# Tile 0 scored in plain float32, GpSimd rounds the first keys, scales and splits the weights and splits one subtile of tile 1, and the early tiles run in a new order

## The chip, the cores and the metric

One core of a Trainium2 chip runs the kernel. Five engines matter here. TensorE (PE) multiplies matrices. VectorE (DVE), ScalarE (ACT) and GpSimd (POOL) work elementwise. SyncE (SP) issues every DMA, one after another from one queue. Each engine works its own list of instructions in order, and semaphores hold an instruction until what it reads is there and the buffer it writes is free. The metric is the device time of one execution in microseconds. The kernel before takes 1856.12 us (median of three runs, 1855.11 to 1856.93).

## The reference

Attention over pooled keys, then a gated feed-forward layer. B = 4, 12288 queries per batch, C = 128, 768 keys per batch, 1024 hidden columns:

```python
kv_pool = kv.reshape(B, H // r, r, W // r, r, C).mean(axis=(2, 4))   # r = 4
k = v = kv_pool.reshape(B, -1, C) @ w_sr                             # 768 keys
s = (q @ k.transpose(0, 2, 1)) / sqrt(C)
a = exp(s - s.max(-1)); a /= a.sum(-1) + 1e-09
x = a @ v
xk = mu_k * x + (1 - mu_k) * x_prev      # x_prev: x of the query before
xr = mu_r * x + (1 - mu_r) * x_prev
out = sigmoid(xr @ w_r) * (maximum(xk @ w_k, 0) ** 2 @ w_v)
```

## The kernel before

The queries run in 97 tiles: 95 of 512 columns and, at the end, two of 256. A tile of 512 has four subtiles of 128 queries. Per subtile PE makes the scores `S` (128x768 in one of three `big` PSUM buffers), DVE takes the row maximum (`nm`), ACT the exponential and its sum (`ex`), and ACT and DVE split the scaled result into a rounded half and a remainder (`f1`, `f2`, tile `pp`). SP transposes `pp` by DMA into `pT` (`tt`). Then PE makes `px` = values x `pT` (`AV0` to `AV5`, 18 matmuls). From `px` come `xk` and `xr`, each split again. PE makes four blocks of hidden columns from `xk` (`ha`, `hb`, PSUM `ph`), ACT and DVE square them (`r`, `k2`, `kh`, `kl`), PE sums them into `pv` (`va`, `vb`) and makes the gate `pz` (`z`).

Almost every product is made of three narrow ones, from operands split into a high and a low part. For the scores of the first tiles these are `ql` x `kbl` (bfloat16), `qh` x `ksh` (a rounded float32) and `qh` x the second half of `kbl`. `ksh`, `kb` and `kd` are the three steps that make the split keys, `qh` and `ql` those that split the queries, `wh` and `wd` (`wx2` for a third copy) those that split the weights `wk`, `wv`, `wr`.

Before the first score the head loads the weights (`L_wk0` and so on), eight blocks of the first 512 key columns (`L_a0` to `L_a7`, tile `kva`) and five groups of the other 256 (`L_b0` to `L_b4`, tile `kvb`). All thirteen key loads share six buffers (`kv`), so the seventh load waits until the first is used. PE sums the `a` blocks into `pk` (`pa0` to `pa7`, two float32 matmuls each), DVE sums the `b` groups (`ab`), PE multiplies these by the key weights (`pk1`, `pk2`), and ACT writes the keys (`ks0` to `ks2`). The rest of the head finds the largest weight (`wa`, `wc`, `wx` to `wg`), prepares the weights on DVE and ACT (`wb`, `wf`, `wu`, `ws`, `wt`, `we`, `wl`, `wq`, `wp`) and prepares the values (`vh`, `vl`, transposed by `tv`). The `id` steps are fillers: two 128-column float32 matmuls each, of a unit matrix with itself, whose result nobody reads.

The order is a table of numbers. Every step has a due time, in `ONCE` for the head and `EARLY` for tiles 0 to 7, and in `WHEN` (plus a period of 19.3 per tile) after that. `Plan` sorts all steps by due time and issues them. The numbers are not checked against the clock: they set nothing but the order on each engine, and a step late on one engine holds whatever stands behind it there.

Of the kernel before, what the change touches and what calls it, by code (L numbers as in the profile page):

```python
# [23 lines left out]
K_SHIFT = 23  # L24
# [49 lines left out]
def tile_kernel(ctx, tc, qT, kv0a, kv0b, kvw, head, w_k, w_v, w_r, outT):  # L74
# [114 lines left out]
    land, sums = {}, {}  # L189
# [50 lines left out]
    def weights(name, w, hi, lo, place, extra):  # L240
# [94 lines left out]
        for i, (c0, c1) in enumerate(parts):  # L335
            @once(f"wh_{name}{i}")
            def _(i=i, c0=c0, c1=c1):
                act.activation(
                    out=hi[:, c0:c1], in_=st["t", i], func=AF.Copy, scale=gain(name)
                )  # L340

            if ENGINE["wd"] == "P":
                @once(f"wz_{name}{i}")
                def _(i=i):
                    act.activation(
                        out=st["t", i], in_=st["t", i], func=AF.Copy, scale=gain(name)
                    )

            @once(f"wd_{name}{i}")
            def _(i=i, c0=c0, c1=c1):  # L350
                if ENGINE["wd"] == "P":
                    pool.tensor_tensor(
                        out=lo[:, c0:c1], in0=st["t", i], in1=hi[:, c0:c1], op=ALU.subtract
                    )
                else:
                    dve.scalar_tensor_tensor(
                        out=lo[:, c0:c1], in0=st["t", i], scalar=gain(name), in1=hi[:, c0:c1],
                        op0=ALU.mult, op1=ALU.subtract,
                    )

            if extra is not None:
                @once(f"wx2_{name}{i}")
                def _(i=i, c0=c0, c1=c1):
                    pool.tensor_copy(out=extra[:, c0:c1], in_=hi[:, c0:c1])
# [19 lines left out]
    def first_keys(ks):  # L384
# [54 lines left out]

        return pks  # L440
# [35 lines left out]
    def batch_prep(b, i0, res):  # L476
# [22 lines left out]
        for n, (c0, c1) in enumerate(PARTS if not later else []):  # L499
            @at(f"ksh{n}")  # L500
            def _(n=n, c0=c0, c1=c1):
                act.activation(
                    out=put("ksh")[:, c0:c1], in_=pks[n][:, 0:c1 - c0], func=AF.Copy, scale=scale / WIN
                )

            @at(f"kb{n}")
            def _(n=n, c0=c0, c1=c1):
                act.activation(
                    out=put("kbl")[:, 0, c0:c1], in_=pks[n][:, 0:c1 - c0], func=AF.Copy,
                    scale=scale / WIN,  # L510
                )

            @at(f"kd{n}")
            def _(n=n, c0=c0, c1=c1):
                dve.scalar_tensor_tensor(
                    out=put("kbl")[:, 1, c0:c1], in0=pks[n][:, 0:c1 - c0], scalar=scale / WIN,
                    in1=res["ksh"][:, c0:c1].bitcast(F32), op0=ALU.mult, op1=ALU.subtract,
                )
# [16 lines left out]
        def _():  # L535
# [5 lines left out]
            dve.reciprocal(ivs, exs)  # L541

# [54 lines left out]

        @at("sv")
        def _():
            dve.reciprocal(xi, xt)  # L600
            dve.tensor_scalar_mul(sk, xi[:, 2:3], X_TOP)
            dve.tensor_copy(out=put("bk"), in_=xt[:, 2:3])
            for i in range(2):
                dve.tensor_scalar(
                    put("s4")[:, 2 * i:2 * i + 2], mix[:, 2 * i:2 * i + 2], xi[:, i:i + 1], exs,
                    op0=ALU.mult, op1=ALU.mult,
                )
# [17 lines left out]
    def plan_tile(i, b, t0, T, at0):  # L625
# [10 lines left out]
        last = max((f"v{x}{f}" for x in "ab" for f in range(NF // 2)), key=places.get)  # L636
        first = min((f"v{x}{f}" for x in "ab" for f in range(NF // 2)), key=places.get)
# [4 lines left out]
        def at(name):  # L642
            def put(fn):
                plan.add(places[name] + base, name, fn, ("tile", i))
# [94 lines left out]
        def _():  # L739
# [4 lines left out]
            act.copy(out=st["qh"], in_=st["qf"])  # L744
# [23 lines left out]
        def products(S, s, c0, c1):  # L768
            ksh, kbl = bps[b]["ksh"], bps[b]["kbl"]
# [8 lines left out]
        for s in range(NSUB):  # L778
# [61 lines left out]
            if opt["TT"][s] == "P":  # L840
# [15 lines left out]
                def _(s=s):  # L856
                    if "pT" not in st:
                        new("pT")
                    act.copy(out=st["pT"][:, s, 0:NK, :], in_=st[f"pm{s}"][:, 0:NK, :])
# [9 lines left out]

            @at(f"f1{s}")  # L870
            def _(s=s):
                pp = new(f"pp{s}")
                rc = st[f"rc{group[s]}"][:, s:s + 1]
                if opt["F1"][s] == "A":
# [20 lines left out]
        for j in range(NK):  # L895
            @at(f"AV{j}")
            def _(j=j):
                vT = bps[b]["vT"]
                name = f"AV{j}"
                if name == av_first:  # L900
                    st["px"] = take("x", name="px")[:, 0:T]
                for m, (w, a) in enumerate(((0, 1), (1, 0), (0, 0))):
# [78 lines left out]

        for f in range(NF // 2):
# [3 lines left out]
            def _(f=f, halves=halves):  # L986
# [3 lines left out]
                st[f"ph{f}"] = ph  # L990
                for i, fs in halves:
# [17 lines left out]
            def _(f=f):  # L1009
                if opt["KV"][f] in "24":  # L1010
# [73 lines left out]
OPT = {'F1': 'AAAA', 'CAST': 'DD', 'KV': '1123', 'T1': 'D', 'TT': 'DDDD'}  # L1084
EARLY_OPT = [{'TT': 'DDDP'}]
# [7 lines left out]
POOLED = ()  # L1093
ENGINE = {'wd': 'D', 'cz': 'P', 'cv': 'P', 'uz': 'P', 'vl': 'P', 'am': 'D', 'mq': 'A', 'qs': 'P'}
# [7 lines left out]
IDLE = 24  # L1102
# [385 lines left out]
```

## Time and profile before

| | us |
|---|---|
| median of three runs | 1856.12 |
| profiled execution, first to last instruction | 1854.3 |
| PE busy | 1839.3 (99%) |
| DVE busy | 1730.9 (93%) |
| ACT busy | 1743.0 (94%) |
| GpSimd busy | 1133.2 (61%) |
| PE waits named in the trace, sum | 5.8 |

PE is busy in nearly the whole span, but a filler counts as busy too. So a reader has to separate PE time into products that the result needs, fillers, and waits. All named waits of PE but two (0.5 us and 0.2 us) lie before 60 us. The time of a run and the span of the profiled execution differ by 1.8 us here, of which the trace says nothing.

### The profile page before, as it was taken

To read this page: it belongs to the slowest core of one execution; us is meant where nothing else is said; L and a number is where in the kernel's file an instruction comes from. 1 tells how busy PE (TensorE), PEld (TensorE's weight loads), DVE (VectorE), ACT (ScalarE), POOL (GpSimd) and SP (SyncE) were. 2 spreads that over 40 slices of the span, in tenths; PEclk is the share of its full clock that TensorE was granted. 3 is DMA by queue.
4 is the path that set the end of the run, shared out by engine and by line. 5 is a ranking of instruction groups with operands and counts; after the bars stand their busy time and mean duration, and the time that the engine had idled before them with its cause. 6 is when DMAs were issued, how large, how long until landed. Compare 5 with 4: busy or idle time off the path is not lost.

```text
span 1854.3 us, 27743 instructions
## 1 busy us (share of the span) xinstructions
PE 1839.3 (99%) x9079; PEld 912.5 (49%) x9185; DVE 1730.9 (93%) x2811; ACT 1743.0 (94%) x2628; POOL 1133.2 (61%) x875
## 2 busy tenths in 40 slices
PE   9999999999999999999999999999999999999999
PEld 6444454444444444444444444444444444444445
DVE  8999999999999999999999999999998999899898
ACT  6999999999999999999999999999999999999997
POOL 1655565666666566666666666656666666666666
PEclk9999999999999999999999999999999999999999
DMA  7677575656667676656666676747565656555462
GB/s 248 142 154 160 130 166 125 129 128 131 135 138 168 142 159 148 134 118 128 137 127 164 142 170 141 161 103 142 123 136 120 128 128 125 120 109 114 91 126 57
DMA packets 654336, 252.52 MB, mean 136 GB/s; under 512 B 612080, under 2 KB 613104, under 8 KB 654192
## 3 DMA queue, kind: packets, MB, share of 16 engines
q1 hardware_dynamic: 654192, 250.75, 63.1%
q8 instruction: 72, 1.18, 0.3%
q14 instruction: 72, 0.59, 0.1%
HBM read 73.34 MB, written 25.17 MB: 53 GB/s over the span
## 4 chain that ended last, share of the span: by engine, by line
PE 89%; ACT 2%; issue 1%; DVE 0%; DVEq 0%; ACTq 0%
PE ph L39 25%; PE pv L39 24%; PE S L39 19%; PE px L39 18%; PE pz L39 3%; ACT rr L39 0%; ACT kh L39 0%; ACT pp L39 0%; PE pk L39 0%; ACT pe L39 0%; ACT kk L39 0%; ACT S L39 0%; ACT xer L39 0%; DVE pp L39 0%; DVE kk L39 0%
## 5 line engine op out<-in xcount | busy, mean ns | idle before, releaser
L39 POOL TENSOR_TENSOR kl<-kk,kh 128x1024 bf16<-128x1024 f32 (+1 forms) x291 | 617.9, 2124 | 129.4 <-ACT kh L39 112.6
L39 ACT ACTIVATE rr<-ph 128x1024 f32<-128x1024 f32 (+1 forms) x388 | 395.8, 1021 | 80.0 <-PE ph L39 76.8
L39 PE MATMUL px<-pT,vT 128*128 128x512 f16 (+1 forms) x1746 | 391.8, 377 | 2.1 <-DMA pT<-pp 2.1
L39 POOL TENSOR_TENSOR xrl<-xr,xrh 128x512 f16<-128x512 f32 (+1 forms) x97 | 144.9, 1494 | 275.1 <-DVE xrh L39 275.1
L39 ACT ACTIVATE kh<-rr 128x1024 f16<-128x1024 f32 (+1 forms) x291 | 306.5, 1055 | 0.7 <-PE pv L39 0.2
L39 PE MATMUL S<-kf,qh 128*128 128x256 f16 x1264 | 304.3, 326 | 0.0
L39 PE MATMUL ph<-xkh,wkl 128*128 128x512 f16 (+1 forms) x776 | 292.0, 377 | 0.4 <-DVE kk L39 0.2
L39 PE MATMUL pv<-kh,wvl 128*128 128x512 f16 (+1 forms) x776 | 291.9, 377 | 0.1
L39 PE MATMUL ph<-xkh,wkh 128*128 128x512 f16 (+1 forms) x776 | 291.9, 377 | 0.0
L39 PE MATMUL pv<-kh,wvh 128*128 128x512 f16 (+1 forms) x776 | 291.8, 377 | 0.0
L39 DVE SCALAR_TENSOR_TENSOR pp<-pe,rc,pp 128x768 f16<-128x768 f32 x289 | 286.9, 1011 | 0.5 <-ACT pp L39 0.5
L39 PEld LDWEIGHTS <-vT 128*128 128x128 f16 x1746 | 170.4, 98 | 205.9 <-issue 3.1
L39 ACT ACTIVATE pp<-pe,rc 128x768 f16<-128x768 f32 x289 | 263.8, 952 | 1.6 <-DVE rc L39 1.6
L39 DVE TENSOR_SCALAR_CACHE_REDUCE pe<-S,gs 128x768 f32<-128x768 f32 x238 | 238.0, 1015 | 25.5 <-PE S L39 25.4
L39 POOL TENSOR_TENSOR ql<-qf,qh 128x512 f16<-128x512 f32 (+2 forms) x97 | 141.9, 1463 | 195.1 <-ACT qh L39 195.1
L39 ACT ACTIVATE pe<-pe,nm 128x768 f32<-128x768 f32 x265 | 248.0, 936 | 0.3 <-DVE pe L39 0.3
L39 PEld LDWEIGHTS <-wkh 128*128 128x128 f16 x1552 | 151.8, 98 | 178.4 <-issue 0.7
L39 DVE TENSOR_TENSOR kk<-ph,rr 128x1024 f32<-128x1024 f32 (+1 forms) x194 | 233.9, 1206 | 3.9 <-ACT rr L39 3.2
L39 PE MATMUL ph<-xkl,wkh 128*128 128x512 f16 (+1 forms) x776 | 228.6, 377 | 0.0
L39 PE MATMUL S<-kf,ql 128*128 128x256 f16 x632 | 205.9, 326 | 4.1
L39 POOL TENSOR_TENSOR xkl<-xk,xkh 128x512 f16<-128x512 f32 (+1 forms) x97 | 145.1, 1496 | 103.0 <-DVE xkh L39 103.0
L39 PE MATMUL pv<-kl,wvb 128*128 128x512 bf16 (+1 forms) x681 | 193.0, 377 | 0.5
(152 smaller groups left out, 2937.5 us busy)
## 6 DMA issues: line engine op xcount, KB each, us to landing
qf<-qT SPq DMA_DIRECT2D x95, 256.0 KB, 3.6
outT<-o SPq DMA_DIRECT2D x95, 256.0 KB, 3.4
qm<-qT SPq DMA_DIRECT2D x78, 256.0 KB, 3.6
kvt<-kvw SPq DMA_DIRECT2D x36, 512.0 KB, 4.9
pT<-pp SPq DMA_TRANSPOSE x383, 4.0
kva<-kv0a SPq DMA_DIRECT2D x8, 512.0 KB, 9.4
kvb<-kv0b SPq DMA_DIRECT2D x3, 512.0 KB, 6.0
land<-moe_w_k SPq DMA_DIRECT2D x2, 512.0 KB, 6.2
```

Of the source, the lines that this page charges most:

```text
L39: return self.tc.keep_in_program_order(op(*args, **kwargs))
```

## The change

Tile 0 takes its scores from the queries and keys as they are, in plain float32: one product of a 128x128 by 128x768 instead of three, and no `qh` and `ql` for it. The split keys are made by GpSimd from the finished `ks`, one instruction for all 768 columns each, where ACT and DVE made them from PSUM in three parts. The weights are scaled in place by GpSimd (`wz`, new), rounded by ACT (`wh`) and the remainder is taken by GpSimd (`wd`, on DVE before). Subtile 0 of tile 1 is scaled (`f00`, new), rounded and split by GpSimd. `sv` is cut in two (`sw` is its later part). The head and tiles 0 to 7 have new due times, and there are 30 fillers where there were 24. `WHEN` and the last two tiles keep theirs. (Branches of the new code for letters other than "S" in `WHOLE` are not taken.)

```diff
@@ weights
+            @once(f"wz_{name}{i}")
+            def _(i=i):
...
+                    {"P": pool, "D": dve}[ON["wz"]].tensor_scalar(
+                        st["t", i], st["t", i], gain(name), 1.0, op0=ALU.mult, op1=ALU.mult
+                    )
             @once(f"wh_{name}{i}")
             def _(i=i, c0=c0, c1=c1):
-                act.activation(
-                    out=hi[:, c0:c1], in_=st["t", i], func=AF.Copy, scale=gain(name)
-                )
+                COPY[ON["wh"]](out=hi[:, c0:c1], in_=st["t", i])
             @once(f"wd_{name}{i}")
             def _(i=i, c0=c0, c1=c1):
...
+                {"P": pool, "D": dve}[ON["wd"]].tensor_tensor(
+                    out=lo[:, c0:c1], in0=st["t", i], in1=hi[:, c0:c1], op=ALU.subtract
+                )
@@ batch_prep
-        for n, (c0, c1) in enumerate(PARTS if not later else []):
-            @at(f"ksh{n}")
...
+        if not later:
+            @at("ksh")
+            def _():
+                COPY[ON["ksh"]](out=put("ksh"), in_=ks)
+            @at("kb")
+            def _():
+                COPY[ON["kb"]](out=put("kbl")[:, 0, :], in_=ks)
+            @at("kd")
+            def _():
+                {"P": pool, "D": dve}[ON["kd"]].tensor_tensor(
+                    out=put("kbl")[:, 1, :], in0=ks, in1=res["ksh"].bitcast(F32), op=ALU.subtract
+                )
@@ plan_tile, products
+            if "S" in whole:
+                pe.matmul(
+                    S[:, c0:c1], lhsT=st["qf"][:, s * P:(s + 1) * P], rhs=bps[b]["ks"][:, c0:c1],
+                    start=True, stop=True,
+                )
+                return
@@ plan_tile, f1 and f2
+            if opt["F1"][s] in "PQR":
+                @at(f"f0{s}")
+                def _(s=s):
+                    rc = st[f"rc{group[s]}"][:, s:s + 1]
+                    pool.tensor_scalar(
+                        st[f"pe{s}"], st[f"pe{s}"], rc, 1.0, op0=ALU.mult, op1=ALU.mult
+                    )
...
+                if opt["F1"][s] in "PQR":
+                    pool.tensor_tensor(out=pp[:, 1, :], in0=pr, in1=pp[:, 0, :], op=ALU.subtract)
+                    return
@@ settings
-OPT = {'F1': 'AAAA', 'CAST': 'DD', 'KV': '1123', 'T1': 'D', 'TT': 'DDDD'}
-EARLY_OPT = [{'TT': 'DDDP'}]
+OPT = {'QH': 'A', 'F1': 'AAAA', 'CAST': 'DD', 'KV': '1123', 'T1': 'D', 'TT': 'DDDD'}
+EARLY_OPT = [{'TT': 'DDDP'}, {'F1': 'PAAA'}]
-IDLE = 24
+IDLE = 30
+WHOLE = "S"
+ON = {'wz': 'P', 'wh': 'A', 'wd': 'P', 'ksh': 'P', 'kb': 'P', 'kd': 'P', 'tx': 'A'}
 ONCE = {
-    "id16": -145.90482, "id17": -144.90482, "id18": -143.90482, "id19": -142.90482,
...
+    "L_wk1": -148.96733, "wb_wk1": -147.93466, "id0": -146.90199, "id1": -145.86932,
```

TensorE, from the start of the program, before (`cs<-ident` is a filler matmul, two to an `id` step; `pk<-kva` an `a` block, two matmuls each; numbers are buffer numbers):

```order
L39 MATMUL cs_96<-ident_64 128x128 x16
L39 MATMUL pk_156<-acc_131,first_71 128x64
L39 MATMUL pk_158<-kva_133,first_71 128x512 x2
L39 MATMUL cs_96<-ident_64 128x128 x6
L39 MATMUL pk_158<-kva_183,first_71 128x512 x2
L39 MATMUL pk_158<-kva_185,first_71 128x512 x2
L39 MATMUL pk_158<-kva_187,first_71 128x512 x2
```

The same place now:

```order
L39 MATMUL cs_100<-ident_64 128x128 x34
L39 MATMUL pk_143<-kva_129,first_71 128x512 x2
L39 MATMUL pk_143<-kva_137,first_71 128x512 x2
L39 MATMUL cs_100<-ident_64 128x128 x6
L39 MATMUL pk_143<-kva_151,first_71 128x512 x2
L39 MATMUL cs_100<-ident_64 128x128 x2
```

Where 16 filler matmuls and then two batches of 6 and 8 stood between the key products, 34 now stand ahead of the first key product, and batches of 6, 2 and 2 between them.

TensorE at the first scores, before (a score of tile 0 in its three parts; `x6` are fillers):

```order
L39 MATMUL cs<-ident 128x128 x6
L39 LDWEIGHTS ql
L39 MATMUL S<-kbl,ql 128x512
L39 MATMUL S<-ksh,qh 128x512
L39 LDWEIGHTS qh
L39 MATMUL S<-kbl,qh 128x512
```

and now, from the last key product (`pk<-acc`, 192 columns) on:

```order
L39 MATMUL pk<-acc,first 128x192
L39 MATMUL S<-ks,qf 128x512
L39 MATMUL S<-ks,qf 128x256
L39 MATMUL S<-ks,qf 128x512
L39 MATMUL S<-ks,qf 128x256
L39 LDWEIGHTS ones
L39 MATMUL all<-tops,ones 128x384
L39 MATMUL S<-ks,qf 128x512
L39 MATMUL S<-ks,qf 128x256
L39 MATMUL S<-ks,qf 128x512
L39 MATMUL S<-ks,qf 128x256
```

No filler stands between the keys and the scores any more, and the eight float32 matmuls of tile 0 (four scores) follow the last key product directly.

SyncE, the last key loads, before (each `kva` or `kvb` load of 128x1024 is 512 KB; `qf` are query tiles):

```order
L39 DMA kva_212<-kv0a 128x1024
L39 DMA kva_214<-kv0a 128x1024
L39 DMA kvb_239<-kv0b 128x1024
L39 DMA kva_251<-kv0a 128x1024
L39 DMA kvb_264<-kv0b 128x1024
L39 DMA kvb_266<-kv0b 128x1024
L39 DMA qf_273<-qT 128x512
```

and now:

```order
L39 DMA kva_256<-kv0a 128x1024
L39 DMA qf_260<-qT 128x512
L39 DMA kvb_270<-kv0b 128x1024
L39 DMA kva_273<-kv0a 128x1024
L39 DMA kvb_284<-kv0b 128x512
L39 DMA kva_292<-kv0a 128x1024
L39 DMA kvb_298<-kv0b 128x1024
L39 DMA qf_334<-qT 128x512
```

The last `a` block (`L_a5`) is now the last load but two; tile 1's queries are loaded ahead of the last five key loads, tile 0's behind them.

## Rows read from the trace of the kernel before

**Rows 1.** The page: DMA issues, count, size, median us from issue to landing.

```profile
kvt<-kvw SPq DMA_DIRECT2D x36, 512.0 KB, 4.9
pT<-pp SPq DMA_TRANSPOSE x383, 4.0
kva<-kv0a SPq DMA_DIRECT2D x8, 512.0 KB, 9.4
```

**Rows 2.** Stretches: length, busy (count) of PE, PEld, DVE, ACT, POOL; clock, DMA, GB/s.

```profile
0.00:100.00 100.00, 94.43 (x474) 55.83 (x482) 90.81 (x169) 80.81 (x133) 39.90 (x46) 1.00 0.71 188
100.00:200.00 100.00, 98.94 (x482) 49.66 (x487) 96.27 (x142) 93.14 (x136) 56.91 (x42) 1.00 0.67 146
200.00:300.00 100.00, 99.63 (x485) 50.02 (x491) 95.03 (x153) 94.49 (x145) 62.55 (x45) 1.00 0.74 164
```

**Rows 3.** Waits of TensorE: us in total, times, longest.

```profile
PE px L39 <- DMA pT<-pp: 2.1, 3, 0.8
...
PE pk L39 <- DVE acc L39: 1.2, 1, 1.2
PE pk L39 <- DMA kva<-kv0a: 0.8, 2, 0.5
```

**Rows 4.** Timeline of TensorE: start, us, operation, count [idle before].

```profile
1.34 6.43 PE L39 MATMUL cs<-ident 128*128 128x128 f32 x32 [1.34 <-POOL xek L39]
...
13.52 5.42 PE L39 MATMUL pk<-kva,first 128*128 128x512 f32 x12 [0.53 <-DMA kva<-kv0a]
...
29.87 0.38 PE L39 MATMUL S<-kbl,ql 128*128 128x512 bf16 x1
...
33.24 0.27 PE L39 MATMUL S<-kbl,ql 128*128 128x256 bf16 x1
...
34.28 0.27 PE L39 MATMUL S<-kbl,ql 128*128 128x256 bf16 x1
...
36.29 1.50 PE L39 MATMUL cs<-ident 128*128 128x128 f32 x12
...
62.48 0.27 PE L39 MATMUL S<-kbl,ql 128*128 128x256 bf16 x1
...
108.28 4.06 PE L39 MATMUL px<-pT,vT 128*128 128x512 f16 x18 [0.47 <-DMA pT<-pp]
```

**Rows 5.** Filler matmuls of TensorE, from 5 to 6 us (first) and 7 to 8 us.

```profile
L39 PE MATMUL cs<-ident 128*128 128x128 f32 x7 | 1.7, 421 | 0.0
L39 PE MATMUL cs<-ident 128*128 128x128 f32 x7 | 0.9, 275 | 0.0
```

**Rows 6.** Timeline of ScalarE.

```profile
26.82 0.59 ACT L39 ACTIVATE ks<-pk 128x512 f32<-128x512 f32 x1
...
34.24 0.90 ACT L39 ACTIVATE pe<-S,nm 128x768 f32<-128x768 f32 x1
...
35.13 1.75 ACT L39 ACTIVATE pp<-pe,rc 128x768 f16<-128x768 f32 x2
```

**Rows 7.** Timeline of VectorE.

```profile
25.02 2.50 DVE L39 TENSOR_REDUCE acc<-kvb 128x64 f32<-128x1024 f32 x2 [0.71 <-DMA kvb<-kv0b]
...
34.55 1.88 DVE L39 TENSOR_REDUCE nm<-S 128x1 f32<-128x768 f32 x2
...
76.12 1.01 DVE L39 SCALAR_TENSOR_TENSOR pp<-pe,rc,pp 128x768 f16<-128x768 f32 x1
```

**Rows 8.** Groups of GpSimd by form: count, busy us, mean ns.

```profile
L39 POOL TENSOR_SCALAR qf<-qf,sq 128x512 f32<-128x512 f32 x78 | 54.3, 696 | 0.0
L39 POOL TENSOR_TENSOR vv<-vs,vv 128x768 f16<-128x768 f32 x1 | 1.6, 1643 | 0.0
L39 POOL CAST wvb<-wvh 128x512 bf16<-128x512 f16 x2 | 1.2, 620 | 0.0
```

**Rows 9.** Timeline of GpSimd.

```profile
76.29 1.87 POOL L39 TENSOR_TENSOR xrl<-xr,xrh 128x512 f16<-128x512 f32 x1 [1.21 <-DVE xrh L39]
...
91.28 1.16 POOL L39 TENSOR_TENSOR xrl<-xr,xrh 128x512 f16<-128x512 f32 x1
```

More of the change, by code (lines that the diff above doesn't have):

```diff
@@ L187, in _ @@
         dve.memset(mtop[:, 2:3], 1.0)
-    land, sums = {}, {}
+    land, sums, scaled = {}, {}, {}
+    COPY = {"A": act.copy, "P": pool.tensor_copy, "D": dve.tensor_copy}
     def gain(name):
@@ L335, in weights @@
         for i, (c0, c1) in enumerate(parts):
-            @once(f"wh_{name}{i}")
-            def _(i=i, c0=c0, c1=c1):
-                act.activation(
-                    out=hi[:, c0:c1], in_=st["t", i], func=AF.Copy, scale=gain(name)
-                )
-            if ENGINE["wd"] == "P":
-                @once(f"wz_{name}{i}")
-                def _(i=i):
+            @once(f"wz_{name}{i}")
+            def _(i=i):
+                scaled[name, i] = st["t", i]
+                if ON["wz"] == "A":
                     act.activation(
@@ L347, in _ @@
                     )
+                else:
+                    {"P": pool, "D": dve}[ON["wz"]].tensor_scalar(
+                        st["t", i], st["t", i], gain(name), 1.0, op0=ALU.mult, op1=ALU.mult
+                    )
+            @once(f"wh_{name}{i}")
+            def _(i=i, c0=c0, c1=c1):
+                COPY[ON["wh"]](out=hi[:, c0:c1], in_=st["t", i])
             @once(f"wd_{name}{i}")
             def _(i=i, c0=c0, c1=c1):
[L351 to L359, printed above, removed]
+                {"P": pool, "D": dve}[ON["wd"]].tensor_tensor(
+                    out=lo[:, c0:c1], in0=st["t", i], in1=hi[:, c0:c1], op=ALU.subtract
+                )
             if extra is not None:
@@ L438, in _ @@
                 )
+        bps[0]["ks"] = ks
         return pks
@@ L497, in batch_prep @@
         exi = one("exi", I32)
-        for n, (c0, c1) in enumerate(PARTS if not later else []):
-            @at(f"ksh{n}")
[L501 to L517, printed above, removed]
+        if not later:
[9 more added lines that the diff above has]
+                    out=put("kbl")[:, 1, :], in0=ks, in1=res["ksh"].bitcast(F32), op=ALU.subtract
                 )
@@ L541, in _ @@
             dve.reciprocal(ivs, exs)
+        if not later and "A" in WHOLE:
+            @at("iv")
+            def _():
+                st["di"] = take("di")
+                pool.tensor_scalar_mul(st["di"], ident, ivs)
+            @at("tw")
+            def _():
+                st["pw"] = take("big", name="pw", shape=[P, 1024 // P, P])
+                for j in range(NK):
+                    pe.matmul(
+                        st["pw"][:, j, :], lhsT=ks[:, j * P:(j + 1) * P], rhs=st["di"], start=True, stop=True
+                    )
+            @at("tx")
+            def _():
+                res["vTw"] = take("vT", name="vTw", shape=[P, NK, P], dtype=F32)
+                COPY[ON["tx"]](out=res["vTw"], in_=st["pw"][:, 0:NK, :])
         @at("vh")
@@ L596, in _, with factors @@
             dve.tensor_reduce(out=xt, in_=st["dm"], axis=AX.X, op=ALU.max)
+        def factors():
+            dve.tensor_scalar_mul(sk, xi[:, 2:3], X_TOP)
+            dve.tensor_copy(out=put("bk"), in_=xt[:, 2:3])
+        if not later:
+            at("sw")(factors)
         @at("sv")
@@ L600, in _ @@
             dve.reciprocal(xi, xt)
-            dve.tensor_scalar_mul(sk, xi[:, 2:3], X_TOP)
-            dve.tensor_copy(out=put("bk"), in_=xt[:, 2:3])
+            if later:
+                factors()
             for i in range(2):
@@ L635, in plan_tile @@
             places, base = WHEN, base_at * PERIOD
-        last = max((f"v{x}{f}" for x in "ab" for f in range(NF // 2)), key=places.get)
-        first = min((f"v{x}{f}" for x in "ab" for f in range(NF // 2)), key=places.get)
+        whole = WHOLE if i == 0 else ""
+        drop = {x for w in whole for x in SPLITS.get(w, ())}
+        kinds = "a" if "V" in whole else "ab"
+        last = max((f"v{x}{f}" for x in kinds for f in range(NF // 2)), key=places.get)
+        first = min((f"v{x}{f}" for x in kinds for f in range(NF // 2)), key=places.get)
         group = {s: min(s | 1, NSUB - 1) if i < PAIRS else NSUB - 1 for s in range(NSUB)}
@@ L643, in put @@
             def put(fn):
+                if name in drop:
+                    return
                 plan.add(places[name] + base, name, fn, ("tile", i))
@@ L743, in _ @@
                 new("qh")
-            act.copy(out=st["qh"], in_=st["qf"])
+            {"A": act.copy, "P": pool.tensor_copy, "D": dve.tensor_copy}[opt["QH"]](out=st["qh"], in_=st["qf"])
         @at("ql")
@@ L768, in products @@
         def products(S, s, c0, c1):
+            if "S" in whole:
+                pe.matmul(
+                    S[:, c0:c1], lhsT=st["qf"][:, s * P:(s + 1) * P], rhs=bps[b]["ks"][:, c0:c1],
+                    start=True, stop=True,
+                )
+                return
             ksh, kbl = bps[b]["ksh"], bps[b]["kbl"]
@@ L787, in _ @@
                 sl = slice(s * P, (s + 1) * P)
+                if "S" in whole:
+                    for c in CHUNKS[1:] if f"SA{s}" in places else CHUNKS:
+                        products(S, s, *c)
+                    return
                 qh, ql = st["qh"][:, sl], st["ql"][:, sl]
@@ L857, in _ @@
                     if "pT" not in st:
-                        new("pT")
-                    act.copy(out=st["pT"][:, s, 0:NK, :], in_=st[f"pm{s}"][:, 0:NK, :])
+                        if "A" in whole:
+                            st["pT"] = take("pT", name="pTw", shape=[P, NSUB, NK, P], dtype=F32)
+                        else:
+                            new("pT")
+                    COPY[opt["F1"][s]](out=st["pT"][:, s, 0:NK, :], in_=st[f"pm{s}"][:, 0:NK, :])
+                if "A" in whole:
+                    continue
                 @at(f"f2{s}")
@@ L873, in _ @@
                 rc = st[f"rc{group[s]}"][:, s:s + 1]
-                if opt["F1"][s] == "A":
+                if opt["F1"][s] in "PQR":
+                    copy = {"P": pool.tensor_copy, "Q": dve.tensor_copy, "R": act.copy}[opt["F1"][s]]
+                    copy(out=pp[:, 0, :], in_=st[f"pe{s}"])
+                elif opt["F1"][s] == "A":
                     act.activation(out=pp[:, 0, :], in_=st[f"pe{s}"], func=AF.Copy, scale=rc)
@@ L882, in _ @@
                 rc = st[f"rc{group[s]}"][:, s:s + 1]
+                if opt["F1"][s] in "PQR":
+                    pool.tensor_tensor(out=pp[:, 1, :], in0=pr, in1=pp[:, 0, :], op=ALU.subtract)
+                    return
                 dve.scalar_tensor_tensor(
@@ L897, in _ @@
             def _(j=j):
-                vT = bps[b]["vT"]
+                vT = bps[b].get("vT")
                 name = f"AV{j}"
@@ L901, in _ @@
                     st["px"] = take("x", name="px")[:, 0:T]
+                if "A" in whole:
+                    pe.matmul(
+                        st["px"], lhsT=bps[b]["vTw"][:, j, :], rhs=st["pT"][:, 0:NSUB, j, :],
+                        start=(name == av_first), stop=(name == av_last),
+                    )
+                    return
                 for m, (w, a) in enumerate(((0, 1), (1, 0), (0, 0))):
@@ L980, in _, with piece @@
             )
+        def piece(name, fs):
+            j, c = divmod(fs.start, 512)
+            return scaled[name, j][:, c:c + P]
         for f in range(NF // 2):
@@ L990, in _ @@
                 st[f"ph{f}"] = ph
+                if "H" in whole:
+                    for i, fs in halves:
+                        pe.matmul(part(ph, i), lhsT=piece("wk", fs), rhs=st["xk"], start=True, stop=True)
+                    return
                 for i, fs in halves:
@@ L1009, in _ @@
             def _(f=f):
+                if "V" in whole:
+                    kk = st[f"kk{f}"] = take("kv", name="kkw")
+                    if opt["KV"][f] in "24":
+                        act.activation(out=kk, in_=st[f"rr{f}"], func=AF.Square, scale=2.0 ** K_SHIFT)
+                    else:
+                        dve.tensor_tensor(out=kk, in0=st[f"ph{f}"], in1=st[f"rr{f}"], op=ALU.mult)
+                    return
                 if opt["KV"][f] in "24":
@@ L1038, in _ @@
                     st["pv"] = take("v", name="pv")[:, 0:T]
+                if "V" in whole:
+                    for i, fs in halves:
+                        pe.matmul(
+                            st["pv"], lhsT=piece("wv", fs), rhs=part(st[f"kk{f}"], i),
+                            start=(first == f"va{f}" and i == 0), stop=(last == f"va{f}" and i == 1),
+                        )
+                    return
                 for i, fs in halves:
@@ L1093 @@
 POOLED = ()
+SPLIT = ()
 ENGINE = {'wd': 'D', 'cz': 'P', 'cv': 'P', 'uz': 'P', 'vl': 'P', 'am': 'D', 'mq': 'A', 'qs': 'P'}
@@ L1101 @@
 KA = 512
-IDLE = 24
+IDLE = 30
+WHOLE = "S"
+SPLITS = {
+    "S": {"qh", "ql"}, "H": {"xkh", "xkl", "hb0", "hb1", "hb2", "hb3"},
+    "V": {f"{x}{f}" for x in ("kh", "kl", "vb") for f in range(4)},
+}
+ON = {'wz': 'P', 'wh': 'A', 'wd': 'P', 'ksh': 'P', 'kb': 'P', 'kd': 'P', 'tx': 'A'}
 WHEN = {
@@ L1137 @@
 ONCE = {
[37 rows of a table removed]
[38 rows of a table added]
+    "kfl": 339.11635,
 }
@@ L1178 @@
     {
[8 rows of a table removed]
-        "xek": 60.09518, "xk": 62.09518, "xkh": 68.09518, "xer": 72.09518, "xr": 82.09518,
[9 rows of a table removed]
-    },
-    {
[7 rows of a table removed]
-        "AV5": 110.09518, "xcr": 114.09518, "xek": 129.09518, "xer": 130.09518, "xk": 137.09518,
-        "xr": 138.09518, "xkh": 149.09518, "xkl": 163.09518, "ha2": 188.49961, "xrh": 188.55182,
[8 rows of a table removed]
-    },
-    {
[8 rows of a table removed]
-        "xk": 188.68235, "xkh": 188.76067, "xkl": 188.81288, "xrh": 189.15226, "xrl": 191.57565,
[8 rows of a table removed]
-    },
-    {
[17 rows of a table removed]
-    },
-    {
[17 rows of a table removed]
-    },
-    {
[7 rows of a table removed]
-        "AV1": 227.56807, "xcr": 227.9118, "xek": 228.59238, "xk": 229.23924, "xer": 230.29038,
[9 rows of a table removed]
-    },
-    {
[7 rows of a table removed]
-        "AV1": 255.83824, "xek": 257.21489, "xck": 258.13266, "xer": 259.5141, "xk": 261.20005,
[9 rows of a table removed]
-    },
-    {
[17 rows of a table removed]
[8 rows of a table added]
+        "xkl": 95.77558, "xcr": 96.80825, "xer": 99.90626, "ha0": 109.20029, "hb0": 111.26563,
[9 rows of a table added]
+    },
+    {
[8 rows of a table added]
+        "xek": 153.60512, "xk": 160.83382, "xkh": 188.42955, "xkl": 188.44101, "xrh": 188.45247,
[9 rows of a table added]
+    },
+    {
[7 rows of a table added]
+        "AV3": 188.80766, "xek": 188.83058, "xcr": 188.86495, "xk": 188.89932, "xer": 188.93370,
+        "xr": 188.94515, "xkh": 189.17431, "xrh": 189.22014, "xkl": 191.03833, "ha1": 200.71005,
[8 rows of a table added]
+    },
+    {
[8 rows of a table added]
+        "xr": 200.17273, "xkh": 209.10874, "xrh": 209.21495, "xrl": 209.85221, "xkl": 209.89470,
[8 rows of a table added]
+    },
+    {
[8 rows of a table added]
+        "xr": 210.31954, "xrh": 210.46823, "xkh": 210.48948, "xkl": 236.58300, "xrl": 237.18739,
[8 rows of a table added]
+    },
+    {
[7 rows of a table added]
+        "AV3": 233.35961, "xer": 233.56108, "xek": 234.16546, "xk": 234.56839, "xcr": 235.77716,
+        "xr": 236.18008, "xkh": 239.40347, "xrh": 243.42912, "xrl": 243.76266, "xkl": 245.18106,
[8 rows of a table added]
+    },
+    {
[8 rows of a table added]
+        "xr": 261.34040, "xrh": 261.36878, "xkh": 264.89826, "xkl": 270.81486, "xrl": 270.85279,
[8 rows of a table added]
+    },
+    {
[17 rows of a table added]
     },
```

333 rows, old and new, of tables (EARLY, ONCE) are left out of this document.

## The prediction

> **What bounds the kernel now.** I read the busy time by stretches first. From 100 us on TensorE is busy 98.9 to 99.7 us of every 100, and so it is in every later stretch of 100 us; the first has 94.4 [rows 2]. VectorE and ScalarE stay under it. So from 100 us on the time is TensorE's work, which this change leaves as it is (`WHEN`), and a difference must arise in the head: the kernel ends earlier by what TensorE loses less there. Next come TensorE's waits: 4.1 us in three rows [rows 3], of which 0.5 lies at 108 us; the 1.34 us at the start, for the unit matrix, is there in any order [rows 4]. The third view is TensorE's timeline in the head [rows 4]: it shows fillers between the work. A filler counts as busy but is lost time like a wait, and 24 `id` steps are 96 instructions there, since a float32 matmul shows as two (16 in the order, x32 in the row).
>
> **What a filler costs.** The first 32 instructions take 6.43 us [rows 4]. They begin at half speed: one lasts 421 ns between 5 and 6 us and 275 ns between 7 and 8 us [rows 5], although the granted clock stands at 1.00. Later 12 take 1.50 us [rows 4]. Neighbours overlap by about 0.15 us (275 ns against a step near 0.12), so a step is (1.50 - 0.15)/11 = 0.122 us, and one `id` (4 instructions) 0.49 us. Six more fillers, all behind the first 32 instructions, add 2.9 us. That is the first term, and no engine hides it, since TensorE works in order.
>
> **What plain float32 costs.** Three key blocks (3 x 1024 columns in float32) take 5.42 us [rows 4], without the overlap 1.72 ns a column, so 768 columns cost 1.32 us. A score in three parts took 34.28 - 33.24 = 1.04 us [rows 4]. Four scores: +1.1 us.
>
> **What can be won back.** The waits behind that first one: 1.2 + 0.8 us before the scores, 1.6 us of `px` behind them [rows 3]. TensorE also drains for 0.15 us at each of these five, another 0.75. That is 4.35 us. If all of it went and nothing came: 2.9 + 1.1 - 4.35 = -0.35 us. So the change can hardly win: more fillers stand where waits stood.
>
> **Up to the first score.** Before, it starts at 29.87 us [rows 4]. Of that 1.34 is the first wait, 72 filler instructions are 6.28 + 40 x 0.122 = 11.2, waits and two drains 2.3, so the work is 15.0 us. Now the same work and 88 filler instructions (6.28 + 56 x 0.122 = 13.1) give 1.34 + 13.1 + 15.0 = 29.5, plus 0.1 for one `wc` step that moves ahead: 29.6 without any wait. The last `a` block (`pa5`) ends some 0.55 us before that, and the keys need 0.59 us on ScalarE behind it [rows 6] and the drain: 29.8.
>
> The loads decide whether there is no wait. The buffer of `L_a5` is free when `pa2` ends; between that and `pa5` stand two blocks (3.5), a filler and two short steps (0.7). `pa5` could start at 27.3, so `pa2` ends at 23.1, and the load is issued then. A load of this size lands 4.9 us later in the later kernel (`kvt`) and 9.4 us later in the median of the head's `kva`, when many were queued [rows 1]. I take 4.9, since only one other load is still under way: it lands at 28.0, a wait of 0.7, and the first score starts at 30.4. `L_b2` is issued right behind; its sum (2.50/2 = 1.25 us [rows 7]) would end at about 29.7, as TensorE gets to `pk1`. With the load as quick as a transpose (4.0 [rows 1]) the wait is nil.
>
> **From the first score to the first `va`.** Before, `va1` of tile 0 follows the score that starts at 62.48 [rows 4]. By then tiles 0, 1, 2 and one subtile of tile 3 are scored, two `px` and three `ph` made. In the new order exactly the same stands before `va1` (that score follows it), so this is a mark at which both can be compared. Before it took 62.48 - 29.87 = 32.6: 24 filler instructions 2.9, waits 1.6, drains 0.5, the `wc` step 0.1 and 0.2 for the first transposed product, so 27.3 of work. Now 27.3 + 1.1 for float32 + 32 filler instructions 3.9 = 32.3, plus new waits. I look for these where a score needs one of three PSUM buffers. One comes back after `nm` (1.88/2 = 0.94) and `ex` (0.90 and its sum, 1.0) [rows 6, 7], 2.0 us after a score ends. In tile 0 two further scores (2.6 us) hide that; in tile 1 two of 1.04 just do; where two `f1` (1.75 [rows 6]) come between on ScalarE, three fillers (1.46) cover all but 0.3. Tile 2's second score needs a buffer that VectorE frees last (`f23`), some 0.4 late. That is 0.7, and the mark comes at 30.4 + 32.3 + 0.7 = 63.4: +0.9. Without the load's wait it is +0.3, and without the buffers' too -0.4. I take the middle, +0.3.
>
> **The steps that GpSimd takes over.** The keys' split must be there at tile 1's first score, 4 x 1.32 + 0.2 = 5.5 us behind the first score. No row shows a copy of 768 float32 values there. The nearest below is 620 ns for 512 [rows 8], so 0.93; above, the subtraction of 768, 1.64. The three steps take 3.5 to 4.9 us and start 0.5 us late (the second part of the keys): ready 0.1 to 1.5 us before they are needed. Cost nothing, at the upper end just. Off VectorE and ScalarE go these three steps, the weights' remainders and one `f1` and `f2`; since TensorE meets its fillers in order anyway, what this buys is only the waits counted above. Tile 0's `qf` is now read by TensorE itself, so SP's load of tile 3's queries waits for the last float32 score, with the transpose of the values queued behind it; but `vl` on GpSimd (behind the three steps) ends later still, so it costs nothing.
>
> **Behind the mark.** The order of tiles 0 to 7 is new to about 330 us. Before it lost 0.7 us more from 100 to 200 us than in the next 100 [rows 2]. I leave that as it is; all of it could go (-0.7), or as much come again (+0.7).
>
> **Sum.** The profiled execution spans 1854.3 us, 1.8 under the median; I put the difference on the median: 1856.12 + 0.3 = 1856.4 us. On this kernel, less than 0.2% (3.7 us) can't be told from no change. The forecast is no change; its own range is 1855.0 to 1858.
>
> **Rivals.** (1) Slower: the last key block is late. For it: the `kva` row's 9.4 us [rows 1] comes from this queue in this stretch, `L_a5` now waits for the third block before it, and VectorE did wait for a `kvb` load at 25 us [rows 7]. Then it lands at 23.1 + 9.4 = 32.5 instead of 27.3, +5.2, and the time is 1856.12 + 0.3 + 5.2 = 1861.6. It decides from a landing after 30.8. Against it: far fewer bytes are in flight then.
>
> (2) Faster: VectorE and ScalarE are what holds the head, and their relief counts in full. Then all that is lost between the first score and the mark (32.6 - 27.3 = 5.3) goes and only float32 is paid: 1856.12 - 5.3 + 1.1 = 1851.9. For it: they are the engines that TensorE's PSUM buffers wait for. Against it: 8 fillers (3.9 us) are written into this stretch, and TensorE must run them.
>
> (3) GpSimd is late. A subtraction of it took 1.87 us when it began 0.17 us after a VectorE instruction with two SBUF inputs (76.12, 1.01 us long), and 1.16 us elsewhere [rows 7, 9]: it ended 1.03 us after that one. From the keys to the remainder that `va1` needs it now has about 24 us of work (copies 1.9, `kd` and `vl` 3.3, four scalings 2.8 at 0.70 [rows 8], `f00` to `f20` 3.6, four remainders 4.6 at 1.16, three query and `xk` splits 3.8, small steps 4) in 32.6 us. If each of 16 met such an instruction, 16 x 0.71 = 11.4, it would be 2.8 us late: 1856.4 + 2.8 = 1859.2. Against it: the maxima, VectorE's main work in half of this stretch, read PSUM. The Trainium skill speaks against the change here. Its page "SBUF — State Buffer" (Who interferes with whom) says that the two engines share one port pair, which the first to start holds for its whole instruction while the other is blocked, a VectorE instruction with two SBUF inputs included. By that rule, the trace agrees at this place, with 0.71 us lost.
>
> **How the numbers follow.** Forecast 0.70, rival 1 0.13, rival 2 0.05, rival 3 0.12. Slower by over 0.2%: nearly all of rival 1, a quarter of rival 3, and 0.04 for a stall in the new order that I did not find, 0.19. Faster: rival 2 and a little, 0.06. Within: 0.75. The range leaves out most of rival 2 and the end of rival 1: 1853.6 to 1861.2.
>
> **What would show it.** In the changed profile: first score at 29.6 to 30.5 us; 120 filler instructions; a float32 score every 1.32 us; `va1` of tile 0 at 62 to 63.5; TensorE's waits in the head under 3 us in all. A first score before 28.5 or after 31.5, a wait for `kva` over 1 us, or waits of TensorE over 2 us between 64 and 330 us would make it wrong.

## The result, and the profile after

The changed kernel takes 1869.85 us (median of 5 runs, 1869.15 to 1870.83), before 1855.87 beside it (5 runs, 1855.11 to 1856.93). The ratio is 1.0076, 95% interval 1.0064 to 1.0088: 14.0 us slower. The forecast was no change, 1856.4, with a range that ended at 1861.2. It was wrong. The profiled execution spans 1868.1 us, 13.8 more than before's.

Stretches of the changed kernel, with the columns of [rows 2]:

```profile
0.00:100.00 100.00, 91.59 (x461) 55.38 (x467) 86.96 (x151) 72.92 (x118) 47.85 (x58) 1.00 0.68 180
100.00:200.00 100.00, 93.90 (x450) 46.48 (x457) 92.89 (x132) 85.59 (x127) 55.45 (x41) 1.00 0.67 146
200.00:300.00 100.00, 98.92 (x478) 49.50 (x485) 96.76 (x152) 95.24 (x143) 58.18 (x41) 1.00 0.69 148
300.00:400.00 100.00, 99.68 (x487) 49.27 (x492) 93.13 (x153) 95.83 (x144) 62.16 (x48) 1.00 0.62 127
```

TensorE (first figure after the length) is busy 2.8, 5.0 and 0.7 us less than before in the first three; then it is full. That is 8.5 of the 13.8 us; most of the rest is work that it has more of in its list, 24 filler instructions and the float32 scores (2.9 and 1.1 us by the prediction's prices). The busy time is lost up to 250 us, most of it between 100 and 200, where the prediction looked least. ScalarE has less to do (1740.3 us busy in the whole run, 1743.0 before), yet TensorE waits more. TensorE's waits between 28 and 300 us, as in [rows 3] (us in total, times, longest):

```profile
PE ph L39 <- DVE pp L39: 3.7, 3, 1.6
PE pz L39 <- DVE xr L39: 1.6, 1, 1.6
PE ph L39 <- ACT pe L39: 1.4, 1, 1.4
PE pk L39 <- DVE acc L39: 1.4, 1, 1.4
PE S L39 <- DVE kk L39: 1.1, 2, 0.7
...
PE px L39 <- DMA pT<-pp: 0.2, 1, 0.2
```

Before, the waits were for transfers (`px` behind `pT`); now most name VectorE. TensorE's timeline, against [rows 4], with the marks of the prediction:

```profile
29.96 0.59 PE L39 MATMUL pk<-acc,first 128*128 128x192 f32 x2 [1.39 <-DVE acc L39]
30.39 2.74 PE L39 MATMUL S<-ks,qf 128*128 128x512 f32 x8
...
57.62 0.38 PE L39 MATMUL ph<-xkh,wkl 128*128 128x512 f16 x1 [1.42 <-ACT pe L39]
...
65.83 0.38 PE L39 MATMUL pv<-kh,wvl 128*128 128x512 f16 x1
```

The first score starts at 30.39, as forecast (30.4). The first `va` of tile 0 (the prediction's mark; its matmuls write `pv`) comes at 65.83 instead of 63.4: 3.35 behind before's mark at 62.48 [rows 4]. So 10.7 of the 14.0 us are lost behind the mark. There TensorE's named waits add up to 8.4 us, all before 330 us, against 0.7 before; the prediction had called over 2 us between 64 and 330 a sign that it is wrong.

What made VectorE late is in its groups by form from 28 to 210 us (count, busy us, mean ns). This is `rc`, the scaling of two sums for each partition, in the kernel before:

```profile
L39 DVE TENSOR_SCALAR rc<-sm 128x2 f32<-128x2 f32 x16 | 3.1, 195 | 0.2 <-ACT pe L39 0.2
```

and in the changed one:

```profile
L39 DVE TENSOR_SCALAR rc<-sm 128x2 f32<-128x2 f32 x16 | 10.9, 682 | 1.3 <-ACT S L39 1.2
```

Sixteen instructions on two numbers take 10.9 us. One of them, in the changed kernel's timeline of VectorE (start, us):

```profile
111.10 1.83 DVE L39 TENSOR_SCALAR rc<-sm 128x2 f32<-128x2 f32 x1
112.96 0.17 DVE L39 RECIPROCAL rc<-rc 128x2 f32<-128x2 f32 x1
113.05 1.80 DVE L39 TENSOR_REDUCE nm<-S 128x1 f32<-128x768 f32 x2
```

GpSimd's timeline there (two instructions make one row):

```profile
108.67 4.24 POOL L39 TENSOR_TENSOR kl<-kk,kh 128x1024 bf16<-128x1024 f32 x2
```

and ScalarE's:

```profile
114.02 0.90 ACT L39 ACTIVATE pe<-S,nm 128x768 f32<-128x768 f32 x1 [1.93 <-DVE nm L39]
```

`rc` begins at 111.10, 0.3 us after the second `kl` subtraction, and ends at 112.93; the subtraction ends at 112.91. The maxima `nm` stand behind `rc` on VectorE, and ScalarE waits 1.93 us for them. In the changed kernel 11 of the 16 two-column `rc` last over 0.3 us, and each has a GpSimd instruction beside it; before there were two such.

### The profile page after: what moved, and what is told of

It reads as the page before. It is cut to its first block, busy times and chain, and to the rows that moved or that the text cites. A ratio compares the mean times of both kernels' runs of the same rounds, so it can differ in the third digit from the quotient of the medians.

```text
span 1868.1 us, 27779 instructions
## 1 busy us (share of the span) xinstructions
PE 1843.9 (99%) x9095; PEld 915.4 (49%) x9201; DVE 1737.7 (93%) x2802; ACT 1740.3 (93%) x2620; POOL 1145.8 (61%) x890
## 4 chain that ended last, share of the span: by engine, by line
PE 87%; ACT 1%; issue 1%; DVE 0%; DVEq 0%; ACTq 0%
PE ph L39 24%; PE pv L39 23%; PE S L39 19%; PE px L39 18%; PE pz L39 3%; ACT rr L39 0%; PE pk L39 0%; ACT kh L39 0%; ACT pp L39 0%; DVE ph L39 0%; ACT S L39 0%; ACT kk L39 0%; DVE pp L39 0%; ACT pe L39 0%; DVE kk L39 0%
```

## The experiments

Theory A: VectorE loses the time, because an `rc` that meets a GpSimd instruction is held until that one ends (called the port below). Rival B: the new order loses it by itself, by waits for PSUM buffers. Rival C: GpSimd has too much to do in the head. Each ratio below is to the kernel before on the same chip, with its 95% interval.

**The disputed cost by itself.** A probe with `pool.tensor_tensor` on 128x1024 seventy times, and small VectorE instructions beside it and then alone.

```
+for k in range(70):
+    pool.tensor_tensor(out=big[2], in0=big[0], in1=big[1], op=ALU.subtract)
+for c in (2, 1, 3):                # ten of each, then RECIPROCAL, TENSOR_REDUCE, TENSOR_TENSOR
+    dve.tensor_scalar(out, src[:, 0:c], 1e-9, 2.0 ** -15, op0=ALU.add, op1=ALU.mult)
```

> A kernel of its own that computes none of the reference: GpSimd runs 70 subtractions of 128x1024 float32 back to back, VectorE beside them ten each of small instructions on 128x2 (or x1, x3) float32, and the same again after GpSimd has ended. Theory A (the small tensor_scalar of `rc` is held up by GpSimd for a whole GpSimd instruction): the two-column tensor_scalar lasts 1 to 2.2 us in the mean beside GpSimd and 0.16 alone; RECIPROCAL and TENSOR_REDUCE, which never lengthened in the trace of the changed kernel, last 0.16 to 0.2 in both halves; the sum of two SBUF operands is held up like the two-column form. The one-column form is open: 0.15 if what ran in the changed kernel (`ex`, 0.155) is typical. Rival (the lengthening has nothing to do with GpSimd, it is a wait for ScalarE's sum that the profile books as work): all forms last 0.14 to 0.2 us in both halves.

VectorE's groups while GpSimd ran:

```profile
L39 DVE TENSOR_SCALAR ts<-src 128x2 f32<-128x2 f32 x10 | 11.9, 1189 | 0.3
L39 DVE TENSOR_TENSOR two<-src 128x2 f32<-128x2 f32 x10 | 10.6, 1064 | 0.3
L39 DVE TENSOR_SCALAR ts<-src 128x3 f32<-128x3 f32 x10 | 10.2, 1015 | 0.3
...
L39 DVE RECIPROCAL rec<-src 128x2 f32<-128x2 f32 x10 | 1.6, 165 | 0.3
L39 DVE TENSOR_REDUCE red<-src 128x2 f32<-128x2 f32 x10 | 1.5, 153 | 0.3
L39 DVE TENSOR_SCALAR ts<-src 128x1 f32<-128x1 f32 x10 | 1.5, 153 | 0.3
```

and after GpSimd had ended:

```profile
L39 DVE TENSOR_SCALAR ts<-src 128x2 f32<-128x2 f32 x10 | 1.7, 169 | 0.3
L39 DVE TENSOR_SCALAR ts<-src 128x3 f32<-128x3 f32 x10 | 1.7, 168 | 0.3
L39 DVE RECIPROCAL rec<-src 128x2 f32<-128x2 f32 x10 | 1.6, 165 | 0.3
L39 DVE TENSOR_TENSOR two<-src 128x2 f32<-128x2 f32 x10 | 1.6, 160 | 0.3
L39 DVE TENSOR_REDUCE red<-src 128x2 f32<-128x2 f32 x10 | 1.5, 153 | 0.3
L39 DVE TENSOR_SCALAR ts<-src 128x1 f32<-128x1 f32 x10 | 1.5, 153 | 0.3
```

Two or three columns of `tensor_scalar`, and two operands in SBUF, are held up by 0.85 to 1.0 us in the mean; one column, RECIPROCAL and TENSOR_REDUCE not at all. The mean hides two cases: one by one, five of the ten two-column instructions last 2.19 to 2.30 us, nearly a whole GpSimd instruction (2.35), and the five between them, which start just as GpSimd goes from one to the next, 0.17. The Trainium skill, "SBUF — State Buffer" (Who interferes with whom), says that the two engines share a port pair, which VectorE takes in a two-port mode or with two SBUF inputs, and that the later one fully blocks; the trace agrees for the forms that were held, and an instruction on two columns is held as well.

**`rc` in single columns.** It does the same work in twice the instructions.

```
-dve.tensor_scalar(rc, sm, 1e-9, 2.0 ** -15, op0=ALU.add, op1=ALU.mult)
+for c in range(s + 1 - s0):        # tiles 0 to 7
+    dve.tensor_scalar(rc[:, c:c + 1], sm[:, c:c + 1], 1e-9, 2.0 ** -15, op0=ALU.add, op1=ALU.mult)
```

> The changed kernel with `rc` of tiles 0 to 7 scaled one column at a time (two instructions of 128x1 in place of one of 128x2), order and engines as they are. Theory A (VectorE held up in `rc`): the 12.8 us of `rc` between 28 and 210 us fall to about 5, TensorE's waits behind 60 us fall from some 8 us to under 3, and the time is 1858 to 1863 us. Rival B (the new order itself loses the time, by cross waits for PSUM buffers): the time stays within 1 us of 1869.9. If the one-column form is held up as well, `rc` stays long and the time stays too, which would tell nothing between them.

1861.67 us (1.0032, 1.0019 to 1.0046): 8.2 of the 14.0 us come back. That is in theory A's range and far from B's. TensorE's named waits behind 60 us fall from 8.4 to 2.8 us. All `rc` fall from 12.8 to 5.4 us, of which one with four columns, from tile 8, has 1.73. The former two-column `rc`, by form from 28 to 210 us:

```profile
L39 DVE TENSOR_SCALAR rc<-sm 128x1 f32<-128x1 f32 x32 | 3.5, 145 | 1.2 <-ACT S L39 1.1
```

and its stretches (columns as above):

```profile
0.00:100.00 100.00, 94.06 (x474) 57.02 (x481) 86.21 (x164) 73.59 (x119) 50.52 (x60) 1.00 0.72 187
100.00:200.00 100.00, 97.33 (x466) 47.97 (x472) 92.75 (x143) 92.01 (x133) 55.31 (x41) 1.00 0.70 150
```

VectorE does 16 instructions more and has 7.4 us less of `rc`; TensorE gains 2.5 and 3.4 us in the two stretches. The same edit for all tiles, and for `s` (`sv`), adds nothing that can be told:

```
-for i in range(2):
-    dve.tensor_scalar(put("s4")[:, 2 * i:2 * i + 2], mix[:, 2 * i:2 * i + 2], xi[:, i:i + 1], exs, ...)
+for i in range(4):
+    dve.tensor_scalar(put("s4")[:, i:i + 1], mix[:, i:i + 1], xi[:, i // 2:i // 2 + 1], exs, ...)
```

> The changed kernel with every `rc` of every tile and the four factors of `sv` made one column at a time. Against the run with `rc` of tiles 0 to 7 alone (1861.7): `s` at 48 us gives back up to 1.3 us on VectorE and the four-column `rc` from tile 8 on up to 1.6 us each, but from 250 us on VectorE isn't waited for, so theory A expects 1860.0 to 1861.7; a time under 1859 would say that the port costs time in the later stretch too.

1861.16 (1.0032, 1.0019 to 1.0045), as theory A expects. And in the kernel before:

> The kernel before with the same edit. Of its 18 `rc` up to 210 us nine met a GpSimd instruction, mostly at that one's end: 4.0 us against 3.1 undisturbed, and TensorE's only waits behind 60 us are 0.4 us. Theory A: no difference, 1855.0 to 1856.0, which would say that it is the new order that brings `rc` and GpSimd together. Under 1853.5 would say that before lost time by the port too.

1856.97 (1.0007, 0.9998 to 1.0016): 1.0 above the range, but not to be told from no difference. There is nothing to gain there, so the change brought this cost.

**Old engines in the new order.**

```
-EARLY_OPT = [{'TT': 'DDDP'}, {'F1': 'PAAA'}]
+EARLY_OPT = [{'TT': 'DDDP'}]
-ON = {'wz': 'P', 'wh': 'A', 'wd': 'P', 'ksh': 'P', 'kb': 'P', 'kd': 'P', 'tx': 'A'}
+ON = {'wz': 'P', 'wh': 'A', 'wd': 'D', 'ksh': 'A', 'kb': 'A', 'kd': 'D', 'tx': 'A'}
```

> The changed kernel in its new order, but the keys' copies on ScalarE, their remainder and the weights' remainders on VectorE, and tile 1's first subtile split as before (ScalarE and VectorE); GpSimd keeps the scaling of the weights. Theory A: the subtractions of the later tiles (`kl`, `ql`, `xkl`) still meet `rc`, so most stays: 1865 to 1872. Rival C (GpSimd has too much to do in the head and what waits for it is late): 1856 to 1862. Rival B: 1869 to 1874, since VectorE and ScalarE have some 8 us more to do.

1874.7 (1.0100, 1.0085 to 1.0115): slower still by 4.9, and outside all three ranges, A's too; B's is nearest. Rival C falls as the main cause: in this order these steps cost more on ScalarE and VectorE than on GpSimd. The two-column `rc` takes 10.4 us there, and eight of the ten that last over 0.3 us run beside a subtraction of the tiles (`kl`, `xkl`, `xrl`, `ql`): these meet `rc` without GpSimd's new steps. With single columns as well:

> The new order with `rc` in single columns, but the keys' copies, the remainders and tile 1's first split on ScalarE and VectorE as before. With two columns this pair of engines cost 4.8 us more than the change (1874.7 against 1869.9), and `rc` showed 12.6 us there too. Theory A: the port costs the same 7 to 9 us whoever does these steps, so 1865.5 to 1868. If GpSimd's new steps were what meets `rc`: 1872 to 1875.

1869.41 (1.0076, 1.0061 to 1.0091): 5.3 us back, less than the 7 to 9 expected, and 1.4 above the range; TensorE there waits for the remainder of `wv` on VectorE (2.0 us) and once 2.4 us behind `rc`.

**Float32 scores alone, in the kernel before.**

```
 def products(S, s, c0, c1):
+    if i == 0:                      # and no qh, ql for tile 0
+        pe.matmul(S[:, c0:c1], lhsT=st["qf"][:, s * P:(s + 1) * P], rhs=bps[b]["ks"][:, c0:c1], start=True, stop=True)
+        return
...
```

> The kernel before in its own order with one part of the change alone: tile 0's four scores in plain float32 (and without its `qh` and `ql`). By the sum of the prediction float32 costs 4 x 0.28 = 1.1 us on TensorE: 1857.0. If its relief of ScalarE and GpSimd counts, or a filler hides it: 1855.4 to 1856.4. Over 1859 would make it a suspect for the loss.

1856.51 (1.0004, 0.9995 to 1.0014): agrees with +1.1, and by the time alone can't be told from none. The traces show it: from the first score to the first `va` TensorE takes 34.63 us (30.84 to 65.47) against 33.62 (29.87 to 63.49) in the kernel before, 1.0 more.

**Fillers**, both times on top of the single-column `rc`.

```
-for j in range(IDLE):
+for j in range(22):                           # without the late ones
+for j in (*range(12), *range(22, IDLE)):      # without the early ones
```

> The changed kernel with single-column `rc` and without the last eight filler steps (`id22` to `id29`, 32 instructions, all behind the first score). By the prediction's price they are 32 x 0.122 = 3.9 us of TensorE's time. If each filler's time is lost: 1857.8. If they stand where TensorE would wait anyway (for `ex` and `nm` to free a PSUM buffer): 1861.7. I expect about half, 1859 to 1860.5.

> The changed kernel with single-column `rc` and without filler steps `id12` to `id21` (40 instructions, 4.9 us, all ahead of the first score). If the loads of the keys decide when the first score starts: it still starts at 29.5 to 30.6 us, TensorE waits for `kva` or `acc` instead, and the time is 1860.5 to 1862. If the fillers do (blocks done sooner free the loads' buffers sooner): the first score at 26 to 28, and the time 1857 to 1859.

1862.39 (1.0037, 1.0023 to 1.0052) and 1862.84 (1.0038, 1.0023 to 1.0053), against 1861.67 with all of them: these fillers cost nothing here, not even the half that was expected of the late ones. TensorE waits in their place. Two rows of TensorE's waits up to 400 us, without the late ones:

```profile
PE S L39 <- ACT pe L39: 2.6, 3, 1.3
PE ph L39 <- ACT pe L39: 2.1, 2, 1.9
```

and without the early ones the first score still starts at 30.01 us.

**The change in the order of before.** The tables `ONCE` and `EARLY` of before, with the new steps at the places of the old ones.

```
-ONCE = {...}; EARLY = [...]; IDLE = 30        # the changed tables
+ONCE = {...}; EARLY = [...]; IDLE = 24        # those of before
+once["ksh"], once["kb"], once["kd"] = (ONCE["ksh1"] + d for d in (0.01, 0.02, 0.03))
+once[f"wz_{w}"] = ONCE[f"wh_{w}"] - 0.2       # each of the five pieces of weights
+once["sw"] = ONCE["sv"] + 0.01; early[1]["f00"] = early[1]["f10"] - 0.1
```

> The change without its order: float32 scores in tile 0, and GpSimd's new steps (the keys' split, the scaling and the remainders of the weights, tile 1's first subtile), written into the order of before at the places where the old steps stood, with that order's 24 filler steps; `rc` in two columns as it is. Rival B, now that the port explains 8.2 of the 14.2 us (the new order costs the other 6): 1854 to 1858, since the steps leave VectorE and ScalarE and nothing else moves. Theory A alone (GpSimd's added work meets `rc` in any order): `rc` between 28 and 210 us over 8 us and 1859 to 1864. If float32 and GpSimd's steps themselves cost the other 6 us: 1861 or more.

1860.07 (1.0026, 1.0015 to 1.0036), two-column `rc` 5.6 us. Neither B's 1854 to 1858 nor A's 8 us of `rc`: of the 14.0 us the parts without the order cost 4.2, the order the other 9.8. Here another small instruction is caught, the two of `s` on VectorE, by GpSimd's new steps; and TensorE waits for VectorE's `pp` after it. VectorE's timeline:

```profile
45.58 2.25 DVE L39 TENSOR_SCALAR s<-mix,xi,exs 128x2 f32<-128x2 f32 x2
```

GpSimd's:

```profile
45.49 1.65 POOL L39 TENSOR_TENSOR pp<-pe,pp 128x768 f16<-128x768 f32 x1
47.11 1.37 POOL L39 TENSOR_SCALAR top<-top,gain 128x512 f32<-128x512 f32 x2
```

and TensorE's:

```profile
52.41 0.28 PE L39 MATMUL S<-kbl,ql 128*128 128x256 bf16 x1 [1.12 <-DVE pp L39]
```

With `rc` in single columns, and then with `s` too:

> The same with `rc` of tiles 0 to 7 one column at a time. By theory A it differs from the kernel with two columns by what `rc` there shows over 3.5 us between 28 and 210 us; if that is 4 to 5 us as before, by under 1 us: 1853.5 to 1857.

> The change in the order of before, with every `rc` and the four factors of `sv` (`s`) in single columns. In that order with two columns `s` took 2.25 us for two at 45.58, until GpSimd's new subtraction `pp` (45.49, 1.65) and its new scaling `top` had ended, and TensorE then waited 1.1 us for `pp` of VectorE. Theory A (what is left of GpSimd's steps is the port too): `s` falls to some 0.6 us for four and the time is 1856.5 to 1857.8, no longer slower than the float32 scores alone (1856.5) by over 1 us. If the steps cost time by themselves (GpSimd later than VectorE was): 1858.5 to 1859.5, as with `rc` alone.

1858.86 (1.0019, 1.0009 to 1.0029) and 1859.77 (1.0021, 1.0012 to 1.0031). Both miss what theory A expected (the second is near its other case, 1858.5 to 1859.5): the four `s` now take 0.82 us, but freeing them gives nothing. So in the old order GpSimd's steps cost 2 to 3 us that small instructions don't explain. The traces put about 1.6 of it between the first score and the first `va` (36.3 us in both, 34.63 with float32 alone). What is left of the port is small there: with `rc` and `s` in single columns, VectorE's instructions between 28 and 250 us last some 2.7 us in all longer than short ones of the same form, in the kernel before some 2.2. What else the steps make wait isn't shown. With single columns the new order costs only 1861.67 - 1858.86 = 2.8 us more than the old one; with two, 1869.85 - 1860.07 = 9.8.

## Why the prediction was wrong

- **Up to the first score: the number right, with luck.** 30.39 against 30.4. The wait was at `pk1` (1.39 instead of 0.7) for the sum of a `kvb` block that landed late, not for `kva`, and the early fillers took 0.8 less than priced; the two cancel. In the other runs with this head order it starts between 30.01 and 30.62. The sum then took +0.3, the middle of its three cases, though the case with a load's wait gave +0.9.
- **What a filler costs: right as a duration, wrong as a term.** 68 filler instructions took the 9.9 us from 1.34 to 11.24 (10.7 by its price), and later 12 take 1.50 as before. But the +2.9 in the sum isn't a loss: 32 or 40 fewer don't make the kernel (with single-column `rc`) faster, since TensorE then waits for loads and PSUM buffers.
- **What plain float32 costs: right.** Two scores (8 instructions) in 2.74 us are 1.3 us for a score, and the run with float32 alone shows +1.0 from the first score to the first `va`.
- **From the first score to the first `va`: too short by 2.4 us.** New waits were put at 0.7; the named ones add up to 3.0, and the 1.42 for `ph` at 57.62 alone is twice the term. A buffer's wait was looked for at the scores, not at `ph`, which needs the same three buffers. With single-column `rc` the mark is at 65.09, so the port has 0.7 of it.
- **The steps GpSimd takes over, "cost nothing": wrong in the order of before**, where float32 and these steps make 1860.07 and float32 alone 1856.51. In the new order they save: 1874.7 with most of them back on ScalarE and VectorE.
- **Behind the mark, left at plus or minus 0.7: this step failed.** 10.7 us were lost there. Of these 8.2 - 0.7 = 7.5 are `rc` behind GpSimd, by the single-column run. The prediction's first paragraph had left the time from 100 us on to TensorE alone; but VectorE was busy 96.27 of 100 us there [rows 2], which leaves little room for instructions that last up to ten times as long.
- **Rival 3 had the mechanism and the wrong side of it.** It took the port from one row of GpSimd [rows 9] and priced GpSimd's delay, 16 x 0.71, which was to end at 1859.2. The rule that it cited works both ways. What was blocked was VectorE, by up to 1.83 us at a time, in an instruction of 0.16 us that no step of the prediction had looked at; and VectorE, in order, passes the delay on to `nm`, `f2` and `xr`, which ScalarE and TensorE wait for. The trace of before already had this side of it, in VectorE's timeline, where an `rc` lasts until `xkl` on GpSimd ends (105.16):

```profile
104.71 0.48 DVE L39 TENSOR_SCALAR rc<-sm 128x2 f32<-128x2 f32 x1
```

- **Rival 2's relief of VectorE doesn't last.** VectorE is busy 87.0 us of the first 100, against 90.8 [rows 2], but in the whole run 1737.7 against 1730.9: the time in which `rc` is held counts as busy and is more than what was taken off.

The 14.0 us divide as far as the runs go: 8.2 are held-up `rc` (paid almost wholly in the new order: single columns give 8.2 there, 1.2 in the old order with the change, none before); some 1 is float32; 2 to 3 show as GpSimd's steps in the old order; and about 2 to 3 are the new order's other waits. By the intervals each of the small parts is uncertain by 1 to 2 us. The last two shares stay open: the rows name waits for `pe`, `pp`, `kk` and `xr`, but no run takes one of them away alone. A mixture of the two orders, one for the head and one for later tiles, wasn't tried. No version here beats the kernel before.

## What to carry to other kernels

Before an order is changed, look for VectorE's small `tensor_scalar` instructions in SBUF with two or more columns, and those with two operands in SBUF, and ask which GpSimd instruction runs beside them: the price is the rest of that instruction and all that stands behind it on VectorE, not the 0.16 us of the row. Writing a `tensor_scalar` one column at a time is a cheap way to find out, and here it cured that part. Don't count a filler that a schedule places as a cost until a run without it is faster.

## What the runs showed of the hardware that was not expected

- A `tensor_scalar` on 128x2 float32 lasted up to 1.83 us in the kernel and 2.30 us in the probe beside a GpSimd subtraction, 0.17 alone; on 128x1 it lasted 0.153 in both halves of the probe. The 128x3 form was held up like the 128x2 (1015 ns against 168).
- RECIPROCAL on the same two columns was never held up (165 ns in both halves), though it reads and writes SBUF as well.
